# Block-sorted attention with a hypernetwork mixer: one batch turned by transposing transfers, and the order of all units laid out anew

## The chip, the cores and the metric

The kernel runs on one core of a Trainium2 chip. A core has a matrix engine (TensorE, PE in the profile; its weight loads are PEld), a vector engine (DVE), an activation engine (ACT), a general engine (GpSimd, POOL), a synchronisation engine (SyncE, SP) that here only issues transfers, and 16 DMA engines that all queues share. Each engine works through its own instructions in order and waits on semaphores for the others. The metric is device time in microseconds (us), the median of several executions; the profile is of one execution.

## What is computed

Inputs are q, k, v (4 batches, 8 heads, 768 positions, 64 wide), a sort_net of 8x8 for each batch and head, and three weight matrices. Cut to what matters:

```python
P = sort_net
for _ in range(5):                      # Sinkhorn
    P = exp(P - max(P, -1)); P /= sum(P, -1) + 1e-9; P /= sum(P, -2) + 1e-9
k_sorted = einsum('bhij,bhjcd->bhicd', P, k_blocks)     # 8 blocks of 96 rows
v_sorted = einsum('bhij,bhjcd->bhicd', P, v_blocks)
attn = softmax(q_b @ k_sorted_b.T / 8)                  # within each block
x = (attn @ v_sorted_b)                                 # 768 x 512 for each batch
wq, wk = x @ w_q, x @ w_k
mixed = (wq @ wk.T / 8) @ x
out = relu(mixed) @ w_out
```

## The kernel before

The program is a list of units, written out by hand in the string ORDER (L18 to L46). A loop at the end (L597 to L607) walks through the list and issues each unit's instructions, so the list fixes the order on every engine: an engine gets its units in the order in which they stand there. An item such as `K12:6` is read as follows: K is the kind of unit, 1 the batch, 2 the part (here a pair of heads), and 6 the first of the PSUM banks it uses (eight banks in all). Capital letters are matrix products on PE. Small letters that follow are the work of another engine on their result, with the engine named: `k12:D:6` is the copy of that result by DVE (D), A is ACT, G GpSimd, S SyncE. The kinds:

- `l`: loads, all issued by GpSimd with conversion to bf16 (L215): `lq0` is q of batch 0, `lp` the two small weights w_q and w_k (tile wqk, L208), `lo` the matrix w_out (tile wo, L210). There are three buffers each for q, k and v.
- `a`, `c`, `p`, `B`, `u`, `i`: the Sinkhorn iterations (a: exponential on ACT; c: sums and divisions on DVE), constants, and the spread of the result over partitions (tile PTR).
- `n`: M, the sorting matrices of a batch (L239). For batch 0 they are made on DVE from PSUM, two heads at a time; for the others on GpSimd from PTR, four heads at a time (`n10`, `n11`). There are two buffers of M, so batch 2 writes where batch 0 was, and batch 3 where batch 1 was.
- `Q`/`q`: q turned; `K`/`k`: k sorted and turned at once by products with M. Twelve small products in each.
- `V`/`v` and `R`: v sorted into tile Vs, then moved into place by six transfers from SBUF to SBUF on SyncE's queue (tile VT). For batch 0 another way is taken: `Y`/`y` sorts and turns, `F`/`f` turns back, with no transfer.
- `S`/`e`: scores and their exponential (seven units for each batch); `P`, then `r` and `x`: weights by values with the row sums, reciprocal, and division into tile X (five units).
- `T`/`t`: X turned on PE into PSUM and copied to tile XT, four units of eight products; each of the four parts is 96x1024 turned to 128x768. The function `u_D` (L356) does the same by one transposing transfer; no unit of the order before calls it.
- `J`/`j`, `d`: x by w_q and w_k in two halves, each taking all four parts of XT; `W`/`w` turns wk, `G`/`g` is wk by x, `H`/`h` the mixing with relu (tile mixT), `O`/`o` the product with w_out, `s` the store. The o units write four output buffers in turn, so an o waits until the store from that buffer has landed.
- `Z`: products on zeros that fill time on PE; `Z09:2` is nine of them.

Of the kernel before, what the change touches and what calls it, by code (L numbers as in the profile page):

```python
# [16 lines left out]
ORDER = """
i02:D Z03:0 lq0 c00:D lk0 a01:A c01:D i00:G i03:G B01:0 p01:A a02:A p00:A:0 c02:D lq1 lv0 a03:A c03:D lv1  # L18
Z010:0 lk1 a04:A c04:D lp a05:A c05:D lk2 Q03:0 lq2 Q02:1 q03:A:0 Q01:2 B00:3 lo q01:D:2 q02:A:1 Q00:0 n03:D:3
lv2 n01:D:3 K03:1 n02:D:3 K01:4 q00:D:0 k03:A:1 lq3 K02:6 n00:D:3 k01:A:4 k02:D:6 S05:0 u00:A:3 S02:4 e05:A:0  # L20
S03:6 n10:G S04:2 e02:A:4 Q13:0 Q11:1 n11:G q13:D:0 e03:A:6 K00:4 q11:D:1 Q10:0 k00:A:4 S06:6 lk3 Q12:1
e06:A:6 S00:4 q12:D:1 q10:A:0 S01:6 e01:A:6 Y03:0 y03:A:0 e04:A:2 Y01:6 Y00:0 y01:D:6 y00:A:0 n20:G F03:3
Z09:2 f03:A:3 e00:A:4 F01:0 F00:1 f01:D:0 V12:2 f00:D:1 Y02:4 v12:A:2 P04:6 n21:G P01:0 r04:D:6 y02:A:4
x04:D:6 P00:2 R15:S r01:D:0 R14:S lv3 K13:4 r00:D:2 x01:D:0 K11:6 k13:A:4 k11:D:6 K10:0 S16:4 x00:D:2 e16:A:4
V11:6 V10:4 v11:A:6 k10:D:0 T00:3 n30:G F02:2 v10:A:4 t00:D:3 R13:S S11:0 f02:D:2 K12:6 R12:S e11:A:0 S10:4
n31:G k12:D:6 R10:S P02:2 e10:A:4 P03:0 R11:S r02:D:2 x02:D:2 S13:6 K20:4 e13:A:6 r03:D:0 T01:2 x03:D:0
k20:A:4 S14:6 t01:D:2 e14:A:6 T03:0 K22:3 t03:A:0 K23:1 k22:D:3 S15:6 T02:5 e15:A:6 k23:D:1 Q23:4 Q20:3
q23:A:4 Q22:6 t02:D:5 q20:D:3 q22:A:6 S12:0 P13:6 e12:A:0 J00:5 r13:D:6 x13:D:6 P10:3 j00:A:5 S24:0 d00:G
W00:5 r10:D:3 e24:A:0 P14:6 x10:D:3 J01:2 S20:0 j01:D:2 S25:3 e20:A:0 r14:D:6 w00:D:5 d01:G W01:2 x14:D:6
Q21:5 e25:A:3 P11:0 q21:D:5 S26:6 w01:D:2 T13:5 r11:D:0 e26:A:6 x11:D:0 V22:2 t13:A:5 V21:6 v22:A:2 P12:4  # L30
v21:D:6 V20:0 T10:2 R24:S r12:D:4 G00:3 v20:D:0 t10:A:2 R23:S K21:6 R22:S G01:3 k21:A:6 x12:D:4 R21:S Q31:0
g00:A:3 Q33:1 R20:S q31:D:0 H00:2 S21:4 R25:S q33:D:1 H02:6 h00:A:2 T11:0 h02:D:6 e21:A:4 T12:1 S22:2 t12:D:1
H01:6 t11:A:0 S23:4 h01:D:6 O00:1 e22:A:2 J11:0 o00:A:1 e23:A:4 K32:6 j11:D:0 K31:1 k32:D:6 d11:G J10:3
k31:D:1 K33:4 j10:A:3 K30:6 W10:3 d10:D k30:A:6 O02:0 k33:D:4 w10:A:3 W11:7 o02:A:0 S36:5 S35:3 w11:D:7 S32:1
e36:A:5 G10:7 e35:A:3 P22:5 e32:A:1 G11:7 r22:D:5 x22:D:5 V32:3 P23:0 v32:A:3 O05:2 g10:D:7 r23:D:0 x23:D:0
R35:S H11:6 o05:A:2 H10:4 R34:S Q30:3 h11:A:6 h10:D:4 T22:0 V30:1 q30:A:3 P24:6 t22:D:0 O11:5 v30:A:1 r24:D:6
x24:D:6 S30:3 o11:D:5 Q32:0 R31:S e30:A:3 P21:6 R30:S P20:1 q32:A:0 r21:D:6 V31:3 x21:D:6 T23:5 v31:A:3 O03:0
r20:D:1 t23:D:5 x20:D:1 S34:6 R32:S o03:A:0 S33:4 T21:3 R33:S e33:A:4 O04:0 t21:D:3 s01:S e34:A:6 S31:1
o04:D:0 H12:3 T20:5 e31:A:1 h12:D:3 O10:6 s02:S P32:0 o10:D:6 P33:2 r32:D:0 O01:4 s10:S r33:D:2 x32:D:0 O15:6
x33:D:2 P34:0 o15:A:6 O14:7 t20:D:5 P31:2 o01:D:4 o14:A:7 J20:5 r31:D:2 s00:S r34:D:0 x34:D:0 J21:4 s12:S  # L40
j20:A:5 x31:D:2 T32:7 d20:G j21:A:4 W20:0 T33:1 d21:G W21:6 w20:D:0 T31:2 t33:D:1 w21:A:6 G20:0 t31:D:2 P30:5
t32:D:7 G21:0 r30:D:5 x30:D:5 O12:7 g20:A:0 H21:0 o12:A:7 H20:2 H22:4 h21:D:0 h20:A:2 T30:6 O13:7 t30:D:6
O22:3 h22:D:4 o13:A:7 J30:2 s11:S o22:A:3 J31:7 j30:D:2 O21:6 d30:D j31:A:7 d31:D W30:7 W31:5 o21:A:6 O23:4
w31:D:5 w30:A:7 G30:7 o23:A:4 O24:6 s21:S G31:7 o24:A:6 O20:4 g30:A:7 H32:6 o20:D:4 H31:1 h32:A:6 O25:5
h31:D:1 s20:S H30:3 o25:A:5 O35:7 h30:D:3 s22:S O34:6 o35:D:7 O31:5 o34:A:6 s35:S O32:7 s34:S o31:A:5 O30:6
s31:S o32:A:7 O33:5 s32:S o30:A:6 s30:S o33:A:5 s33:S  # L46
"""


# [595 lines left out]
```

## Time and profile before

| | |
|---|---|
| runs | 109.33, 109.36 and 109.76 us, median 109.36 |
| profiled execution | 109.27 us |
| its span from the first to the last instruction seen | 107.4 us |
| input read and output written | 20.19 MB and 6.29 MB |
| dummy products Z | 22 of 1475 matrix products |

The rows in the prediction come from several views: the head of the page; busy time by stretches; the order of time, where a row has start, duration, engine, line, operation, output and input tiles, count, and in brackets how long the engine stood idle ahead of it and what ended that; groups by line and shape, with busy us in all, then ns of one; and the transfers with KB of each and median us from issue to landing. A matmul's duration includes the time that it takes to run through the array, so what one costs in a dense stretch is read from the starts of successive rows, not from their durations.

### The profile page before, as it was taken

The page shows a single profiled execution, that of the slowest core. Times are in us where ns is not written, and L with a number is a line of the kernel's source. Part 1 is how long each engine was busy: PE and PEld are TensorE (multiplying, and loading weights), DVE is VectorE, ACT ScalarE, POOL GpSimd, SP SyncE. Part 2 cuts the span into 40 slices and gives each one's busy share as a digit, 9 for nine tenths or more (in the row PEclk, how much of TensorE's full clock was granted, in tenths as well). Part 3 has the DMA queues.
Part 4 walks back from the last instruction along what each step waited for, and adds up shares of the span by engine and source line. Part 5 has one row for each costly group of instructions (what it writes and reads, how often), then busy time and mean ns, then how long its engine had stood idle before and what let it go on. Part 6 is the DMA issues. An engine that isn't in the chain of part 4 may idle for free.

```text
span 107.4 us, 3466 instructions
## 1 busy us (share of the span) xinstructions
PE 91.2 (85%) x1475; PEld 61.4 (57%) x1486; DVE 72.3 (67%) x143; ACT 68.8 (64%) x99; POOL 28.4 (26%) x47
## 2 busy tenths in 40 slices
...
DMA  0999999999999999999999400323974503145982
GB/s 3 100 198 205 203 205 205 203 204 205 186 204 215 228 233 243 205 205 203 207 209 263 85 6 0 101 55 96 359 279 166 240 0 148 50 198 206 362 310 98
DMA packets 18879, 19.04 MB, mean 177 GB/s; under 512 B 1840, under 2 KB 16944, under 8 KB 18864
## 3 DMA queue, kind: packets, MB, share of 16 engines
...
q14 instruction: 4, 0.03, 0.1%
HBM read 20.19 MB, written 6.29 MB: 247 GB/s over the span
## 4 chain that ended last, share of the span: by engine, by line
PE 43%; DMA 24%; DVE 15%; POOL 8%; issue 4%; ACT 3%; DVEq 0%; SPq 0%; POOLq 0%; ACTq 0%
PE ps L143 43%; DMA Vn<-in_v_dram 17%; DMA VT<-Vs 7%; DVE X L344 6%; POOL M L239 2%; DVE mixT L410 2%; POOL Qn L215 2%; DVE Rall L339 1%; DVE Vs L149 1%; ACT Vs L147 1%; ACT E L315 1%; DVE ot L149 1%; POOL Kn L215 1%; DVE KT L149 1%; POOL Vn L215 1%
## 5 line engine op out<-in xcount | busy, mean ns | idle before, releaser
L315 ACT ACTIVATE E<-ps 96x960 bf16<-96x960 f32 (+1 forms) x28 | 24.4, 902 | 2.3 <-PE ps L143 2.1
L143 PE MATMUL ps<-wo,mixT 128*128 128x512 bf16 x86 | 22.4, 379 | 0.5
L344 DVE TENSOR_TENSOR X<-ps,Rall 96x896 bf16<-96x896 f32 (+1 forms) x20 | 19.8, 1000 | 0.4
L147 ACT COPY ot<-ps 128x512 f32<-128x512 f32 x18 | 10.6, 586 | 10.2 <-PE ps L143 10.1
L371 POOL COPY qD<-qkT 64x384 bf16<-64x384 bf16 x5 | 2.5, 503 | 43.9 <-ACT qkT L147 31.2
L143 PEld LDWEIGHTS <-mixT 128*128 128x128 bf16 x96 | 8.3, 98 | 8.6 <-issue 1.0
L143 PE MATMUL ps<-VT,E 96*128 96x65 bf16 x256 | 10.5, 193 | 1.3 <-DMA VT<-Vs 1.2
L149 DVE CAST KT<-ps 128x768 bf16<-128x768 f32 x10 | 9.4, 952 | 2.8 <-PE ps L143 2.8
L143 PEld LDWEIGHTS <-E 96*128 96x128 bf16 x256 | 9.3, 97 | 2.9 <-issue 1.7
L143 PE MATMUL ps<-fil 128*128 128x512 bf16 x21 | 9.1, 607 | 2.0 <-DVE fil L191 1.2
L143 PEld LDWEIGHTS <-KT 64*128 64x128 bf16 (+1 forms) x288 | 8.5, 98 | 4.1 <-issue 1.9
L147 ACT CAST KT<-ps 128x768 bf16<-128x768 f32 x10 | 7.9, 798 | 3.8 <-PE ps L143 3.7
L410 DVE TENSOR_SCALAR mixT<-ps 128x1024 bf16<-128x1024 f32 x8 | 9.8, 1222 | 0.5 <-PE ps L143 0.4
L147 ACT CAST Vs<-ps 128x1024 bf16<-128x1024 f32 x7 | 7.0, 1019 | 4.3 <-PE ps L143 3.8
L143 PE MATMUL ps<-QT,KT 64*128 64x96 bf16 x256 | 9.1, 204 | 0.5 <-ACT KT L147 0.5
L143 PE MATMUL ps<-idb,X 96*128 96x96 bf16 x128 | 8.0, 207 | 0.6 <-DVE X L344 0.6
L143 PE MATMUL ps<-idb,Qn 128*64 128x128 bf16 x192 | 7.5, 225 | 1.0 <-DMA Qn<-in_q_dram 0.9
L239 POOL TENSOR_TENSOR M<-PTR,m_p 128x512 bf16<-128x512 bf16 x6 | 7.8, 1310 | 1.3 <-PE ps L143 1.3
L143 PE MATMUL ps<-M,Kn 128*64 128x128 bf16 x192 | 7.2, 221 | 0.8 <-DVE X L344 0.4
L143 PEld LDWEIGHTS <-Qn 128*64 128x64 bf16 x192 | 6.2, 113 | 2.6 <-DMA Qn<-in_q_dram 1.9
L143 PEld LDWEIGHTS <-X 96*128 96x128 bf16 x128 | 6.2, 98 | 2.2 <-issue 0.6
L339 DVE RECIPROCAL Rall<-ps 96x14 f32<-96x14 f32 (+1 forms) x20 | 4.3, 223 | 4.7 <-PE ps L143 4.6
...
## 6 DMA issues: line engine op xcount, KB each, us to landing
out_dram<-ot SPq DMA_DIRECT2D x9, 512.0 KB, 2.8
Qn<-in_q_dram POOLq DMA_DIRECT2D x4, 768.0 KB, 18.5
Kn<-in_k_dram POOLq DMA_DIRECT2D x4, 768.0 KB, 22.2
Vn<-in_v_dram POOLq DMA_DIRECT2D x4, 768.0 KB, 21.8
VT<-Vs SPq DMA_DIRECT2D x18, 132.0 KB, 5.8
...
wo<-in_moe_w_out_dram POOLq DMA_DIRECT2D x1, 512.0 KB, 25.1
wqk<-in_moe_w_q_dram POOLq DMA_DIRECT2D x1, 64.0 KB, 20.6
```

The costliest lines, as they stand in the source:

```text
L143: nc.tensor.matmul(o, w, x, is_transpose=t, start=start, stop=stop, skip_group_check=True)
L147: nc.scalar.copy(o, i)
L149: nc.vector.tensor_copy(o, i)
L215: nc.gpsimd.dma_start(out=t[b % NIN][:, h0:h1].rearrange("p h r d -> p h (r d)"), in_=src[b, h0:h1].rearrange("h (p r) d -> p h (r d)", p=P))
L239: ENG[e].tensor_tensor(out=M[b % 2][:, h0:h0 + hn], in0=src.unsqueeze(2).to_broadcast([P, hn, SP, NB]), in1=m_p.unsqueeze(1).unsqueeze(3). ...
L315: nc.scalar.activation(E[b % 2][:, n, 0:2 * w * BLK].rearrange("p (t a c) -> p a t c", a=2, c=BLK), PS[0:BLK, bank:bank + 2, 0:w * BLK].re ...
L339: nc.vector.reciprocal(Rall[:, b, n, :, 0:w], avps(bank, w)[:, :, :, D])
L344: nc.vector.tensor_mul(xo.rearrange("p (a t d) -> p a t d", a=2, d=D), avps(bank, w)[:, :, :, 0:D], Rall[:, b, n, :, 0:w].unsqueeze(3).to_ ...
L371: nc.gpsimd.tensor_copy(o, i)
L410: nc.vector.tensor_relu(o, i)
```

## The change

Only ORDER changes. Three things differ in it. The units T30 to T33 and t30 to t33 are gone, and D30 to D33 on SyncE stand in their stead. The order of the units and loads, the engine of many copies, and the PSUM banks are all dealt out anew. There are 28 dummy products instead of 22. The lines that matter here:

```diff
-i02:D Z03:0 lq0 c00:D lk0 a01:A c01:D i00:G i03:G B01:0 p01:A a02:A p00:A:0 c02:D lq1 lv0 a03:A c03:D lv1
-Z010:0 lk1 a04:A c04:D lp a05:A c05:D lk2 Q03:0 lq2 Q02:1 q03:A:0 Q01:2 B00:3 lo q01:D:2 q02:A:1 Q00:0 n03:D:3
-lv2 n01:D:3 K03:1 n02:D:3 K01:4 q00:D:0 k03:A:1 lq3 K02:6 n00:D:3 k01:A:4 k02:D:6 S05:0 u00:A:3 S02:4 e05:A:0
-S03:6 n10:G S04:2 e02:A:4 Q13:0 Q11:1 n11:G q13:D:0 e03:A:6 K00:4 q11:D:1 Q10:0 k00:A:4 S06:6 lk3 Q12:1
...
-k20:A:4 S14:6 t01:D:2 e14:A:6 T03:0 K22:3 t03:A:0 K23:1 k22:D:3 S15:6 T02:5 e15:A:6 k23:D:1 Q23:4 Q20:3
-q23:A:4 Q22:6 t02:D:5 q20:D:3 q22:A:6 S12:0 P13:6 e12:A:0 J00:5 r13:D:6 x13:D:6 P10:3 j00:A:5 S24:0 d00:G
...
-j20:A:5 x31:D:2 T32:7 d20:G j21:A:4 W20:0 T33:1 d21:G W21:6 w20:D:0 T31:2 t33:D:1 w21:A:6 G20:0 t31:D:2 P30:5
-t32:D:7 G21:0 r30:D:5 x30:D:5 O12:7 g20:A:0 H21:0 o12:A:7 H20:2 H22:4 h21:D:0 h20:A:2 T30:6 O13:7 t30:D:6
-O22:3 h22:D:4 o13:A:7 J30:2 s11:S o22:A:3 J31:7 j30:D:2 O21:6 d30:D j31:A:7 d31:D W30:7 W31:5 o21:A:6 O23:4
...
+i02:D lq0 lv0 c00:D a01:A c01:D i00:G i03:G B01:0 a02:A Z014:1 p00:A:0 c02:D lk0 lv1 a03:A p01:A c03:D lq1 lk1
+a04:A c04:D Q02:1 lq2 Z03:0 Q01:0 a05:A c05:D Q03:2 Z03:7 q03:A:2 Q00:7 q02:A:1 q01:D:0 B00:2 q00:A:7 n03:D:2
+n01:D:2 Y03:0 n02:D:2 Y01:6 n00:D:2 y03:A:0 Y02:3 u00:D:2 y01:A:6 Y00:0 n10:G y02:A:3 y00:D:0 F01:7 F03:6
+n11:G f01:D:7 K01:0 f03:A:6 K00:2 k01:D:0 K02:4 lp K03:6 k02:A:4 k00:D:2 S02:0 e02:A:0 F00:4 k03:D:6 n21:G
...
+x03:D:2 V10:6 q12:A:0 x02:D:4 v10:A:6 Q10:1 T00:0 P04:2 q10:D:1 t00:A:0 R11:S K12:6 r04:D:2 x04:D:2 R15:S
+K13:4 Q11:0 k12:D:6 n31:G k13:A:4 R13:S Q13:1 K11:2 R10:S q13:D:1 T02:4 R14:S T03:7 lv2 t02:A:4 T01:1 t03:D:7
+R12:S Z08:6 t01:A:1 lo q11:A:0 k11:A:2 Q22:7 S16:0 S15:5 q22:D:7 e16:A:0 K10:2 e15:A:5 S13:0 n30:G J01:7
+e13:A:0 J00:5 j01:D:7 lk2 k10:A:2 S14:0 j00:D:5 Q21:7 e14:A:0 lq3 W00:5 q21:D:7 Q20:2 w00:D:5 S12:3 lv3 d00:D
+q20:D:2 W01:0 e12:A:3 V21:6 lk3 P13:1 w01:A:0 G00:5 v21:A:6 r13:D:1 d01:G x13:D:1 S11:3 G01:5 e11:A:3 S10:6
...
+W20:4 P32:0 w20:D:4 O12:5 o13:A:3 r32:D:0 x32:D:0 P31:6 o12:A:5 G20:3 r31:D:6 s11:S x31:D:6 H12:4 D32:S S30:0
+G21:3 e30:A:0 h12:D:4 O11:2 D31:S P34:0 o11:A:2 P30:6 r34:D:0 O14:4 g20:A:3 x34:D:0 r30:D:6 D33:S O10:0
+x30:D:6 o14:A:4 H21:1 o10:D:0 H22:3 D30:S H20:6 h21:A:1 O15:5 h20:D:6 h22:A:3 s10:S O23:0 o15:A:5 O21:7 s12:S
+J31:1 o21:A:7 J30:5 j31:A:1 O20:7 d31:G j30:A:5 o23:A:0 d30:G W30:5 O24:1 o20:D:7 w30:D:5 s20:S W31:7 o24:D:1
...
```

What the transposing unit issues, unchanged in the code:

```python
nc.sync.dma_start_transpose(out=XT[b % 2][:, n, :].rearrange("p (i c) -> p i c", i=NB),
                            in_=X[b % 2][:, n].rearrange("p i m -> p (i m)"))
```

More of the change, by code (lines that the diff above doesn't have):

```diff
@@ L17 @@
 ORDER = """
-i02:D Z03:0 lq0 c00:D lk0 a01:A c01:D i00:G i03:G B01:0 p01:A a02:A p00:A:0 c02:D lq1 lv0 a03:A c03:D lv1
-Z010:0 lk1 a04:A c04:D lp a05:A c05:D lk2 Q03:0 lq2 Q02:1 q03:A:0 Q01:2 B00:3 lo q01:D:2 q02:A:1 Q00:0 n03:D:3
-lv2 n01:D:3 K03:1 n02:D:3 K01:4 q00:D:0 k03:A:1 lq3 K02:6 n00:D:3 k01:A:4 k02:D:6 S05:0 u00:A:3 S02:4 e05:A:0
-S03:6 n10:G S04:2 e02:A:4 Q13:0 Q11:1 n11:G q13:D:0 e03:A:6 K00:4 q11:D:1 Q10:0 k00:A:4 S06:6 lk3 Q12:1
-e06:A:6 S00:4 q12:D:1 q10:A:0 S01:6 e01:A:6 Y03:0 y03:A:0 e04:A:2 Y01:6 Y00:0 y01:D:6 y00:A:0 n20:G F03:3
@@ L23 @@
[L23 to L26, printed above, removed]
-k20:A:4 S14:6 t01:D:2 e14:A:6 T03:0 K22:3 t03:A:0 K23:1 k22:D:3 S15:6 T02:5 e15:A:6 k23:D:1 Q23:4 Q20:3
@@ L28 @@
-q23:A:4 Q22:6 t02:D:5 q20:D:3 q22:A:6 S12:0 P13:6 e12:A:0 J00:5 r13:D:6 x13:D:6 P10:3 j00:A:5 S24:0 d00:G
[L29 to L37, printed above, removed]
@@ L38 @@
-r20:D:1 t23:D:5 x20:D:1 S34:6 R32:S o03:A:0 S33:4 T21:3 R33:S e33:A:4 O04:0 t21:D:3 s01:S e34:A:6 S31:1
-o04:D:0 H12:3 T20:5 e31:A:1 h12:D:3 O10:6 s02:S P32:0 o10:D:6 P33:2 r32:D:0 O01:4 s10:S r33:D:2 x32:D:0 O15:6
-x33:D:2 P34:0 o15:A:6 O14:7 t20:D:5 P31:2 o01:D:4 o14:A:7 J20:5 r31:D:2 s00:S r34:D:0 x34:D:0 J21:4 s12:S
-j20:A:5 x31:D:2 T32:7 d20:G j21:A:4 W20:0 T33:1 d21:G W21:6 w20:D:0 T31:2 t33:D:1 w21:A:6 G20:0 t31:D:2 P30:5
-t32:D:7 G21:0 r30:D:5 x30:D:5 O12:7 g20:A:0 H21:0 o12:A:7 H20:2 H22:4 h21:D:0 h20:A:2 T30:6 O13:7 t30:D:6
@@ L43 @@
-O22:3 h22:D:4 o13:A:7 J30:2 s11:S o22:A:3 J31:7 j30:D:2 O21:6 d30:D j31:A:7 d31:D W30:7 W31:5 o21:A:6 O23:4
-w31:D:5 w30:A:7 G30:7 o23:A:4 O24:6 s21:S G31:7 o24:A:6 O20:4 g30:A:7 H32:6 o20:D:4 H31:1 h32:A:6 O25:5
-h31:D:1 s20:S H30:3 o25:A:5 O35:7 h30:D:3 s22:S O34:6 o35:D:7 O31:5 o34:A:6 s35:S O32:7 s34:S o31:A:5 O30:6
-s31:S o32:A:7 O33:5 s32:S o30:A:6 s30:S o33:A:5 s33:S
+i02:D lq0 lv0 c00:D a01:A c01:D i00:G i03:G B01:0 a02:A Z014:1 p00:A:0 c02:D lk0 lv1 a03:A p01:A c03:D lq1 lk1
+a04:A c04:D Q02:1 lq2 Z03:0 Q01:0 a05:A c05:D Q03:2 Z03:7 q03:A:2 Q00:7 q02:A:1 q01:D:0 B00:2 q00:A:7 n03:D:2
@@ new lines @@
+n01:D:2 Y03:0 n02:D:2 Y01:6 n00:D:2 y03:A:0 Y02:3 u00:D:2 y01:A:6 Y00:0 n10:G y02:A:3 y00:D:0 F01:7 F03:6
+n11:G f01:D:7 K01:0 f03:A:6 K00:2 k01:D:0 K02:4 lp K03:6 k02:A:4 k00:D:2 S02:0 e02:A:0 F00:4 k03:D:6 n21:G
+S01:2 F02:5 e01:A:2 f00:D:4 S06:6 S04:0 n20:G f02:D:5 e04:A:0 S00:2 V12:4 e00:A:2 S05:0 v12:D:4 e06:A:6 P00:2
+e05:A:0 P01:6 r00:D:2 S03:4 x00:D:2 V11:0 e03:A:4 r01:D:6 P03:2 x01:D:6 v11:A:0 P02:4 r03:D:2 Q12:0 r02:D:4
+x03:D:2 V10:6 q12:A:0 x02:D:4 v10:A:6 Q10:1 T00:0 P04:2 q10:D:1 t00:A:0 R11:S K12:6 r04:D:2 x04:D:2 R15:S
@@ new lines @@
+K13:4 Q11:0 k12:D:6 n31:G k13:A:4 R13:S Q13:1 K11:2 R10:S q13:D:1 T02:4 R14:S T03:7 lv2 t02:A:4 T01:1 t03:D:7
+R12:S Z08:6 t01:A:1 lo q11:A:0 k11:A:2 Q22:7 S16:0 S15:5 q22:D:7 e16:A:0 K10:2 e15:A:5 S13:0 n30:G J01:7
+e13:A:0 J00:5 j01:D:7 lk2 k10:A:2 S14:0 j00:D:5 Q21:7 e14:A:0 lq3 W00:5 q21:D:7 Q20:2 w00:D:5 S12:3 lv3 d00:D
+q20:D:2 W01:0 e12:A:3 V21:6 lk3 P13:1 w01:A:0 G00:5 v21:A:6 r13:D:1 d01:G x13:D:1 S11:3 G01:5 e11:A:3 S10:6
+g00:D:5 P14:0 e10:A:6 H01:2 r14:D:0 V20:4 x14:D:0 h01:A:2 H00:6 P12:0 h00:A:6 O02:2 r12:D:0 x12:D:0 v20:A:4
```

13 lines of the change are left out of this document (added).

## The prediction

> **What bounds the kernel now.** I read the page's head first, then busy time by stretches of 5 us, then the order of time on TensorE and GpSimd, then what waited for whom.
>
> ```profile
> span 107.4 us, 3466 instructions
> PE 91.2 (85%) x1475; PEld 61.4 (57%) x1486; DVE 72.3 (67%) x143; ACT 68.8 (64%) x99; POOL 28.4 (26%) x47
> DMA  0999999999999999999999400323974503145982
> ```
>
> ```profile
> 15.00:20.00 5.00, 3.71 (x114) 3.04 (x114) 1.71 (x4) 4.84 (x8) 0.75 (x1) 1.00 1.32 204
> 20.00:25.00 5.00, 2.98 (x46) 2.28 (x48) 0.96 (x1) 4.16 (x6) 0.89 (x1) 0.85 1.32 205
> 25.00:30.00 5.00, 4.70 (x55) 2.96 (x54) 1.29 (x2) 1.64 (x3) 4.39 (x4) 0.81 1.50 195
> 40.00:45.00 5.00, 3.75 (x106) 3.24 (x104) 2.76 (x5) 4.29 (x6) 0.00 (x0) 1.00 1.24 227
> 50.00:55.00 5.00, 4.95 (x110) 4.56 (x111) 4.87 (x8) 4.04 (x6) 0.00 (x0) 1.00 1.32 205
> ```
>
> The columns after the stretch are busy us of PE, weight loads, DVE, ACT and POOL, then the granted clock. There are two regimes. From 45 us PE has hardly a gap (4.95 of 5). Before that it starves: DMA is full and loads arrive one at a time. So what counts is how much matmul work is done when the dense part begins, and how much is left. The boundary is the unit P13 (batch 1, weights by values):
>
> ```profile
> 40.84 0.39 PE L143 MATMUL ps<-QT,KT 64*128 64x96 bf16 x10
> 44.44 0.59 PE L143 MATMUL ps<-VT,E 96*128 96x65 bf16 x14 [1.23 <-DMA VT<-Vs]
> 98.05 5.35 PE L143 MATMUL ps<-wo,mixT 128*128 128x512 bf16 x23
> ```
>
> P13 starts at 44.44, after 1.23 us of waiting for batch 1's sorted V. The reason lies on GpSimd's queue, which carries both the loads and the multiplications n (L239) that make the sorting matrix M:
>
> ```profile
> 1.27 1.13 POOL L215 DMA_DIRECT2D Qn<-in_q_dram  x1 [0.82 <-POOLq L629]
> 2.40 0.89 POOL L215 DMA_DIRECT2D Kn<-in_k_dram  x1
> 5.82 1.76 POOL L215 DMA_DIRECT2D Vn<-in_v_dram  x2
> 25.31 0.88 POOL L215 DMA_DIRECT2D Qn<-in_q_dram  x1 [3.28 <-DMA Vn<-in_v_dram]
> 26.20 2.57 POOL L239 TENSOR_TENSOR M<-PTR,m_p 128x512 bf16<-128x512 bf16 x2
> ```
>
> Batch 1's M is made only at 26.20, because the load of q3 ahead of it waited 3.28 us for v1 to land; V1 and its VT transfers follow from there.
>
> **When loads land.** The views of the three input tiles give issue to landing (minimum, median, maximum; first Qn, then Kn, then Vn):
>
> ```profile
> DMA to landing us min/median/max: 7.7/18.5/25.2
> DMA to landing us min/median/max: 10.5/22.2/25.2
> DMA to landing us min/median/max: 15.0/21.8/27.3
> ```
>
> The minimum of each is its batch 0: q0 at 1.27+7.7 = 9.0, k0 at 2.40+10.5 = 12.9 and v0, the fourth load, at 5.82+15.0 = 20.8. So a load takes 3.95 us. The new order of loads is q0, v0, k0, v1, q1, k1, q2, wqk, v2, wo, k2, q3, v3, k3: v0 12.9, k0 16.9, v1 20.8, q1 24.8, k1 28.7, q2 32.7.
>
> ```profile
> wqk<-in_moe_w_q_dram POOLq DMA_DIRECT2D x1, 64.0 KB, 20.6
> Qn<-in_q_dram POOLq DMA_DIRECT2D x4, 768.0 KB, 18.5
> VT<-Vs SPq DMA_DIRECT2D x18, 132.0 KB, 5.8
> out_dram<-ot SPq DMA_DIRECT2D x9, 512.0 KB, 2.8
> ```
>
> By bytes the two halves of wqk cost 0.66 us (33.4), v2 another 3.95 (37.4), and batch 1's six VT transfers up to 6·132/768 of a load, 4.1 us. That puts v2 between 37.4 and 41.5. I take 40.5, since these transfers leave when v10 is done, about 29, and mostly run ahead of v2.
>
> **The change part by part.** *Early order.* n10 and n11 now stand ahead of every load that can wait, so V1 follows v1 (20.8) instead of a waiting load. The new order then runs load by load to V21, first user of v2. Engines allow about the same time. Between K12 (28.7 plus some 0.8 for its bank) and V21, ACT has six evacuations of 0.8, four exponentials and a short one:
>
> ```profile
> L315 ACT ACTIVATE E<-ps 96x960 bf16<-96x960 f32 x24 | 22.5, 971 | 1.6 <-PE ps L143 1.5
> L147 ACT CAST KT<-ps 128x768 bf16<-128x768 f32 x10 | 7.9, 798 | 3.8 <-PE ps L143 3.7
> ```
>
> 4.8+3.9+0.5 = 9.2, to 38.7 without a gap. So V21 starts at 40.5, bounds 38.7 and 42.5 (loads at their latest, plus 1 us of waits).
>
> What is done by then, against before at 44.44? Batch 0's attention and its T0, and V1, Q1, K1 and three of Q2, in both. The new order has J00, J01, W00, W01 more, and S11, S10 and three K2 less. Starts of successive PE rows price these:
>
> ```profile
> 73.49 0.60 PE L143 MATMUL ps<-QT,KT 64*128 64x96 bf16 x20
> 74.02 0.52 PE L143 MATMUL ps<-idb,X 96*128 96x96 bf16 x8
> 40.05 0.86 PE L143 MATMUL ps<-M,Kn 128*64 128x128 bf16 x24
> 81.25 1.46 PE L143 MATMUL ps<-XT,wqk 128*128 128x384 bf16 x8
> 82.55 0.51 PE L143 MATMUL ps<-idb,X 96*128 96x96 bf16 x8
> 82.89 0.39 PE L143 MATMUL ps<-idb,qkT 128*96 128x128 bf16 x4
> 83.11 0.51 PE L143 MATMUL ps<-idb,X 96*128 96x96 bf16 x8
> ```
>
> S is (74.02−73.49)/2 = 0.27, K (40.84−40.05)/2 = 0.40, J (82.55−81.25)/2 = 0.65, T 0.34, W 0.22. So 1.74 more against 1.74 less: equal work, reached 44.44−40.5 = 3.9 us sooner (bounds 1.9 and 5.7). The price after that point is taken as unchanged: engine letters and banks are dealt out anew, but DVE loses evacuations and ACT gains some, with the sum of both smaller. I bound this re-dealing by ±1 us, about one exponential's length of extra or saved wait.
>
> *Turning X3.* T30 to T33 leave PE: 4·0.34 = 1.4 us in the dense part, so on the path. Their four DVE copies leave too, 0.54 each, beside PE work:
>
> ```profile
> L149 DVE COPY XT<-ps 128x768 bf16<-128x768 bf16 x12 | 6.5, 544 | 0.2 <-PE ps L143 0.2
> L344 DVE TENSOR_TENSOR X<-ps,Rall 96x896 bf16<-96x896 f32 x16 | 17.2, 1079 | 0.3
> L344 DVE TENSOR_TENSOR X<-ps,Rall 96x512 bf16<-96x512 f32 x4 | 2.7, 684 | 0.1
> 77.96 1.89 PE L143 MATMUL ps<-wo,mixT 128*128 128x512 bf16 x8
> 79.69 0.41 PE L143 MATMUL ps<-VT,E 96*128 96x65 bf16 x8
> L301 SPq DMA_DIRECT2D VT<-Vs x18: 546/598/1452, 30.4 to 74.0; - x18
> DMA to landing us min/median/max: 2.3/5.8/7.6
> ```
>
> In their place SyncE issues D32, D31, D33, D30, each 96x1024 bf16, 196 KB. J31's first product reads the part that D30 writes. D30 waits for x30. From P30's start, DVE still has x34 (0.68) and x30 (1.08) with two short reciprocals, about 2.9 us after P30's start with its matmuls. PE meanwhile has P30, O14, O10, H21, H22, H20, O15, O23 and O21: five O at (79.69−77.96)/2 = 0.87, P30 and three H about 1.3, together 5.7. So D30 has 2.8 us of cover. No row here shows a transposing transfer. The nearest one from SBUF to SBUF on this queue is VT<-Vs, 2.3 us at its fastest for 132 KB, which by bytes makes 3.4; 2.3 would be hidden, 7.6 (its slowest, under full load) would stall 4.8. I take 3.4: 0.6 us of stall. It can't gain, for PE has other work. Behind J31 all of PE waits; behind D30 on SyncE stands s10, which frees the slot that o23 on ACT writes, with w31 and g30 behind that.
>
> [...]
>
> *Fillers.* The dummy products Z go from 22 to 28, all before 35 us where PE starves. They cost nothing while loads set the pace; without that cover, 0.2 to 0.4 us each.
>
> *Loads late in the order.* lv2 now stands behind n31 on GpSimd, which needs K12 and K13 (about 30.3) and takes 1.3: issue at 31.6, while q2 and wqk fill the queue to 33.4. No gap, margin 1.8 us. lk2 stands behind n30 (K10, about 36): 37.6, with v2 and wo still moving.
>
> **Sum.** Against the profiled execution, 109.27 us (its span 107.4, 1.87 around it): −3.9 −1.4 +0.6 = 104.6. It lies 0.09 under the median of the runs, 109.36, so 104.7. The tail behind PE (last copy, last store) stays as it is. Terms at their ends: −5.7−1.4−1.0 gives 101.3; −1.9−1.4+1.0 with no stall 107.1.
>
> **Rivals.** *The transfers queue up (slower).* If a transposing transfer holds the queue c us and the four run one after another, D30 ends 4c after D32's start, which stands six O (5.2) and about 2.3 us of S30, G21, P34, P30 and three H ahead of J31; the stall is 4c−7.5. With the gain of 5.3 this turns slower from c = 3.2. At the VT median, c = 5.8, the stall is 15.7 and the time 104.1+15.7 = 119.8. For it: nothing is measured for such a transfer, and 5.8 is what an SBUF to SBUF transfer took here. Against: those ran against full loads, several at once, and from 60 us on the DMA row shows mostly under half. [...] Chance 0.22.
> *Only D30 is late.* Latency up to 7.6 with overlap among the four: 104.1+4.8 = 108.9, middle 107. Chance 0.12.
> *The load-paced stretch slips.* PE in the gaps drops to the clock of the rows at 20 to 30 us (0.85, 0.81), where eight fillers took 3.21 us, 0.4 each, against 0.87/4 = 0.22 for the same shape later:
>
> ```profile
> 24.21 3.21 PE L143 MATMUL ps<-fil 128*128 128x512 bf16 x8 [0.22 <-issue]
> ```
>
> From K12 to V21 stand some 7 us of PE work; at 1.8 times that, V21 comes 5.6 us later, past its load, and lv2 misses its margin: 104.7+5.6 = 110.3, and half as much, 107.5, if the clock recovers midway. Against: 15 to 20 us kept 1.00 with 3.71 us busy, and the new order is denser there. Chance 0.11.
>
> **How the numbers follow.** Forecast 104.7, chance 0.55; its own range 101.3 to 107.1. All of it is faster by over 0.5% (0.55 us, about what a measurement of this kernel can tell from no change). The late D30 adds 0.11 faster and 0.01 same, the slipping stretch 0.03, 0.04 and 0.04, the queue 0.01 same and 0.21 slower: faster 0.69, same 0.06, slower 0.25. The range runs from 102.0 to 111.0 and leaves out most of the queueing case and a sliver below.
>
> **What would show it.** M of batch 1 made by 19 us; V21 near 40.5 and P13 without a VT wait; PE dense from there, last matmul near 98.5; D30 landing under 4 us after issue and J31 waiting less than 1 us. The early step is wrong if V21 starts after 43, or the clock is under 0.9 in 28 to 40 us. The forecast falls if SyncE issues the D's more than 3 us apart with x ready, or if J31 waits over 4 us.

## The result, and the profile after

| kernel | runs | median | ratio to before, 95% interval |
|---|---|---|---|
| before | 109.24 to 109.76 us | 109.34 us | |
| changed | 104.92, 105.29, 105.76, 107.26 us | 105.53 us | 0.962 [0.958, 0.966] |

The change makes the kernel 3.8 us faster by the medians; 104.7 had been forecast. The execution profiled with the result is the one of 107.26 us, in which the granted clock fell behind a wait of PE (first fence); ratios and times below leave such executions out (which leaves one of six for a1_T and c4_k0 and two of six for c3_s12 and d1_noZ8, and the traces of a1_T, c2_Dlast, c4_k0 and d1_noZ8 are of executions left out), and the same kernel, run once more as a0_same, is read from an undisturbed execution of 105.50 us.

The profiled execution of the changed kernel: one row of the order of time on PE, and two stretches (columns as before; the granted clock is the third number from the end).

```profile
40.72 0.61 PE L143 MATMUL ps<-Vn,M 128*128 128x128 bf16 x8 [1.91 <-DMA Vn<-in_v_dram]
```

```profile
40.00:45.00 5.00, 4.28 (x68) 3.17 (x69) 1.75 (x3) 2.59 (x3) 0.29 (x1) 0.73 1.29 207
45.00:50.00 5.00, 4.78 (x46) 2.76 (x44) 2.39 (x5) 3.31 (x4) 0.00 (x0) 0.59 1.31 202
```

In a0_same (line numbers of the kernels run as experiments are one or two lower, so L141 here is L143 in the rows of before) the same stretches and the ones shown of before read:

```profile
15.00:20.00 5.00, 4.49 (x102) 3.92 (x104) 4.55 (x6) 4.05 (x6) 4.99 (x6) 1.00 1.32 204
20.00:25.00 5.00, 4.18 (x106) 3.44 (x106) 3.98 (x7) 4.77 (x7) 1.15 (x1) 1.00 1.32 204
25.00:30.00 5.00, 4.08 (x113) 3.65 (x111) 4.94 (x9) 3.43 (x5) 0.33 (x1) 1.00 1.32 205
...
40.00:45.00 5.00, 4.35 (x84) 3.17 (x84) 2.65 (x5) 3.46 (x5) 0.17 (x1) 1.00 1.29 206
...
50.00:55.00 5.00, 4.82 (x115) 3.60 (x115) 3.89 (x7) 4.57 (x7) 0.00 (x0) 1.00 1.25 235
```

PE is busy 4.18 of 5 us between 20 and 25 us, where it was 2.98, and at the full clock, where it was 0.85. DMA is as full as before (1.32): the loads did not get faster, the work stands in a better order behind them. GpSimd's order of time in a0_same shows how:

```profile
14.46 2.58 POOL L237 TENSOR_TENSOR M<-PTR,m_p 128x512 bf16<-128x512 bf16 x2 [5.14 <-ACT KT L145]
...
30.93 0.95 POOL L213 DMA_DIRECT2D Vn<-in_v_dram  x1
```

M of batch 1 is made at 14.46, not 26.20, and lv2 is issued at 30.93. PE's order of time in a0_same, at the four places that matter:

```profile
40.65 0.61 PE L141 MATMUL ps<-Vn,M 128*128 128x128 bf16 x8 [1.50 <-DMA Vn<-in_v_dram]
41.09 0.60 PE L141 MATMUL ps<-VT,E 96*128 96x65 bf16 x14
...
59.70 0.60 PE L141 MATMUL ps<-VT,E 96*128 96x65 bf16 x14 [1.23 <-DMA VT<-Vs]
...
87.22 1.46 PE L141 MATMUL ps<-XT,wqk 128*128 128x384 bf16 x8 [1.21 <-DMA XT<-X]
...
93.60 6.27 PE L141 MATMUL ps<-wo,mixT 128*128 128x512 bf16 x28
```

V21 starts at 40.65 behind v2, P13 follows without a wait, the first P of batch 2 waits 1.23 us for its VT transfers, and J31 waits 1.21 us for D30. From the boundary to PE's end, one stretch of each kernel, first before, then a0_same:

```profile
44.44:103.44 59.00, 57.98 (x846) 37.93 (x856) 45.18 (x73) 38.99 (x58) 5.75 (x12) 1.00 0.63 168
```

```profile
40.65:99.87 59.22, 56.05 (x856) 36.91 (x863) 40.89 (x66) 42.24 (x60) 5.20 (x11) 1.00 0.81 193
```

So the dense part is as long as it was (59.22 against 59.00): PE has 1.93 us less to do in it, and stands idle 3.17 us instead of 1.02. In lengths, the gain of 3.7 us in span (103.7 against 107.4) is the 3.8 us by which the dense part begins sooner. That does not make the transfers worth nothing: c1_T2 below begins its dense part as early and turns X3 on PE, and its dense part is longer.

### The profile page after: what moved, and what is told of

Same layout as the page of the kernel before. It is cut to its first block, busy times and chain, and to the rows that moved or that the text cites. A ratio compares the mean times of both kernels' runs of the same rounds, so it can differ in the third digit from the quotient of the medians.

```text
span 105.5 us, 3413 instructions
## 1 busy us (share of the span) xinstructions
PE 90.5 (86%) x1450; PEld 61.0 (58%) x1460; DVE 68.6 (65%) x138; ACT 70.4 (67%) x100; POOL 28.4 (27%) x47
## 4 chain that ended last, share of the span: by engine, by line
PE 49%; DMA 33%; POOL 6%; ACT 3%; issue 3%; DVE 2%; POOLq 0%; DVEq 0%
PE ps L143 49%; DMA Kn<-in_k_dram 20%; DMA Vn<-in_v_dram 9%; DMA XT<-X 4%; ACT E L315 2%; DVE X L344 2%; POOL Vn L215 2%; POOL Qn L215 1%; POOL M L239 1%; POOL Kn L215 1%; ACT ot L147 1%; POOL E L196 0%; DVE Rall L339 0%; POOL idb L187 0%; POOL VT L202 0%
## 5 line engine op out<-in xcount | busy, mean ns | idle before, releaser
L315 ACT ACTIVATE E<-ps 96x960 bf16<-96x960 f32 (+1 forms) x28 | 23.8, 899 | 3.7 <-PE ps L143 3.6
L143 PE MATMUL ps<-wo,mixT 128*128 128x512 bf16 x88 | 22.9, 386 | 0.7 <-issue 0.5
L143 PEld LDWEIGHTS <-mixT 128*128 128x128 bf16 x96 | 8.5, 99 | 9.4 <-issue 1.4
L147 ACT COPY ot<-ps 128x512 f32<-128x512 f32 x15 | 8.8, 587 | 6.3 <-PE ps L143 4.1
L143 PE MATMUL ps<-VT,E 96*128 96x65 bf16 x256 | 11.1, 197 | 0.9 <-ACT E L315 0.7
L149 DVE COPY ot<-ps 128x512 f32<-128x512 f32 x9 | 6.1, 683 | 8.6 <-PE ps L143 8.5
L143 PEld LDWEIGHTS <-E 96*128 96x128 bf16 x256 | 9.8, 100 | 2.9 <-issue 1.4
L143 PEld LDWEIGHTS <-KT 64*128 64x128 bf16 (+1 forms) x288 | 8.6, 99 | 3.9 <-issue 2.2
L147 ACT CAST KT<-ps 128x768 bf16<-128x768 f32 x12 | 9.4, 807 | 1.7 <-PE ps L143 1.7
L408 ACT ACTIVATE mixT<-ps 128x1024 bf16<-128x1024 f32 x8 | 8.1, 1024 | 3.3 <-PE ps L143 3.2
L143 PE MATMUL ps<-QT,KT 64*128 64x96 bf16 x256 | 9.5, 209 | 0.1
L149 DVE CAST KT<-ps 128x768 bf16<-128x768 f32 x8 | 7.5, 955 | 2.2 <-PE ps L143 2.2
L143 PE MATMUL ps<-fil 128*128 128x512 bf16 x26 | 8.2, 468 | 0.2 <-issue 0.2
L143 PE MATMUL ps<-idb,Qn 128*64 128x128 bf16 x192 | 7.9, 221 | 0.2 <-ACT Vs L147 0.2
L143 PE MATMUL ps<-M,Kn 128*64 128x128 bf16 x192 | 7.2, 221 | 0.7 <-DMA Kn<-in_k_dram 0.7
L149 DVE COPY QT<-ps 128x768 bf16<-128x768 bf16 x11 | 6.0, 549 | 2.7 <-PE ps L143 2.6
L143 PE MATMUL ps<-Vn,M 128*128 128x128 bf16 x72 | 5.9, 229 | 1.9 <-DMA Vn<-in_v_dram 1.9
```

Source lines behind the costliest of these rows:

```text
L143: nc.tensor.matmul(o, w, x, is_transpose=t, start=start, stop=stop, skip_group_check=True)
L147: nc.scalar.copy(o, i)
L149: nc.vector.tensor_copy(o, i)
L315: nc.scalar.activation(E[b % 2][:, n, 0:2 * w * BLK].rearrange("p (t a c) -> p a t c", a=2, c=BLK), PS[0:BLK, bank:bank + 2, 0:w * BLK].re ...
L408: nc.scalar.activation(o, i, ACT.Relu)
```

## Experiments

The kernel before was run beside them each time, with medians of 109.36 to 109.61 us.

**a0_same**, the changed kernel again.

> The changed kernel once more, so that the others have it beside them. Mean of its undisturbed runs near 105.3 us. If its profile has the clock at 1.00 from 40 to 50 us, the idle time of PE ahead of V21 (1.9 us in the first profile) and the wait for D30 (about 1.3 us) should be there all the same, for they come from transfers and not from the clock.

Measured: 105.11 to 106.16 us, median 105.66, ratio 0.964 [0.960, 0.968]. The waits for v2 (1.50 us) and for D30 (1.21 us) are there at the full clock, as expected. The result stands, and this is the measure for the variants below.

**a1_T**, the transposes of the last batch put back on PE, with one bank:

```diff
-H12:4 D32:S S30:0
+H12:4 T32:2 t32:D:2 S30:0
...
-H22:3 D30:S H20:6 h21:A:1 O15:5
+H22:3 H20:6 h21:A:1 T30:2 t30:D:2 O15:5
```

> The changed kernel with X of the last batch turned on PE again (T30 to T33 and their four copies on DVE), everything else as it is. My theory: PE gets 1.4 us of work back and loses the wait of 1.2 to 1.4 us for D30, so the time is within 0.7 us of the changed kernel (104.6 to 106.0), and J31 no longer waits for a transfer. The rival, that the transposing transfers carry a good part of the gain: 1.4 us slower or more. The rival, that they cost: over 0.7 us faster.

Measured: 108.24 us, one execution. It does not tell the theories apart, for my choice of bank 2 made a wait of its own:

```profile
85.45 0.28 PE L141 MATMUL ps<-qD,Ab 64*128 64x256 bf16 x1 [1.02 <-DVE XT L147]
```

H21 writes banks 1 and 2 and had to wait until the copy t33 had emptied bank 2. c1_T2 below does it with other banks.

**b1_D**, the order of before with T3 and t3 alone replaced by the four transfers:

```diff
-T32:7 d20:G j21:A:4 W20:0 T33:1 d21:G W21:6 w20:D:0 T31:2 t33:D:1
+D32:S d20:G j21:A:4 W20:0 D33:S d21:G W21:6 w20:D:0 D31:S
...
-h20:A:2 T30:6 O13:7 t30:D:6 O22:3
+h20:A:2 D30:S O13:7 O22:3
```

> The kernel before with the four transposing transfers alone, its order otherwise kept. In its profile x30 ends at 86.76 and the first unit that needs D30 starts at 89.58, which leaves 2.8 us, and T30 leaves that stretch, so D30 at 3 to 4.3 us stalls PE by 0.5 to 1.9 us, against 1.4 us of PE work saved. My theory: within 0.8 us of 109.3. If the transfers carry the change: 107.9 or less. If they queue up one after another: over 110.

Measured: 111.19 us, ratio 1.014 [1.011, 1.016], 1.4% slower. The expectation of no change within 0.8 us missed. The first J of batch 3 in PE's order of time:

```profile
91.93 1.46 PE L141 MATMUL ps<-XT,wqk 128*128 128x384 bf16 x8 [2.45 <-DMA XT<-X]
```

D30 was issued at 87.6, 1.9 us ahead of the end of the products that cover it, and took 4.3 us. The time lies where the queueing theory had put it (over 110), but the transfers did not queue: the one issued just ahead of D30 landed in 2.7 us. So the transfers alone are a loss where their cover is short; what makes D30 take 4.3 us is taken up below.

**a2_V21**, V21 put behind P13, G00 and S11 so that PE has work while v2 is still on its way:

```diff
-V21:6 lk3 P13:1 w01:A:0 G00:5 v21:A:6 r13:D:1 d01:G x13:D:1 S11:3 G01:5 e11:A:3 S10:6
+lk3 P13:1 w01:A:0 G00:5 r13:D:1 d01:G x13:D:1 S11:3 V21:6 e11:A:3 G01:5 v21:A:6 S10:6
```

> The changed kernel with V21 moved behind P13, G00 and S11, which need no load. If PE's idle stretch ahead of V21 is lost time on the path, as I hold, these 1.3 us of work fill it and the time falls by 0.8 to 1.5 us; the clock should also drop less often. If the stretch behind V21 is paced by ACT or by later loads, nothing changes (within 0.4 us).

Measured: 105.20 us, ratio 0.961 [0.958, 0.964]: 0.5 us below a0_same's 105.66, less than expected, and with intervals that overlap. The wait for v2 is gone, but half of it comes back one bank later:

```profile
42.91 0.39 PE L141 MATMUL ps<-QT,KT 64*128 64x96 bf16 x10 [0.85 <-ACT Vs L145]
```

S10 uses the bank that V21 has just filled and waits for ACT to empty it.

**c1_T2**, T30 to T33 on PE in other banks, two of the copies on ACT, and O15 ahead of J31:

```diff
-H12:4 D32:S S30:0
+H12:4 T32:2 t32:D:2 S30:0
...
-r30:D:6 D33:S O10:0 x30:D:6 o14:A:4
+r30:D:6 O10:0 T33:5 x30:D:6 t33:A:5 o14:A:4
...
-H22:3 D30:S H20:6 h21:A:1 O15:5
+H22:3 H20:6 T30:5 t30:D:5 h21:A:1
```

> The changed kernel with X of the last batch turned on PE, a second time: the first such kernel put three of the turns into banks that H21 and the relu copies wanted, and PE waited 1 us on a copy there, which says nothing of the transfers. Here the turns go to banks 2 and 5, two copies go to ACT, and O15 moves behind O21. My theory: 1.4 us more PE work against 1.2 to 1.4 us less waiting for D30, so within 0.8 us of the changed kernel's undisturbed runs (105.6), and no wait of J31 for a transfer. If the transfers carry part of the gain: 107 or more with PE free of waits there.

Measured: 107.96 us, ratio 0.986 [0.979, 0.992]. My theory, within 0.8 us of the changed kernel, missed. With the new order kept, the transfers are worth 2.3 us by the medians (107.96 to 105.66), not the forecast's 0.8, though the width of the interval leaves some 0.7 us either way. In the trace the last block of O starts at 95.50, against 93.60. Both traces stand at the same unit at 77.45; from there to that block PE is busy 16.81 us here and 14.58 in a0_same, and idle 1.24 and 1.57. Of the 2.23 us of busy time 1.4 are what the forecast gave the T's. Part of the idle time is that the last mixing comes late behind the copies on DVE and ACT:

```profile
85.78 1.04 PE L142 MATMUL ps<-wo,mixT 128*128 128x512 bf16 x3 [0.43 <-ACT mixT L407]
87.20 1.90 PE L142 MATMUL ps<-wo,mixT 128*128 128x512 bf16 x8 [0.38 <-DVE mixT L409]
88.94 1.65 PE L142 MATMUL ps<-XT,wqk 128*128 128x384 bf16 x8
```

These two waits, 0.8 us together, stand in place of the 1.21 us for D30. Where the T's were put back is my choice, so part of the 2.3 may belong to it.

**c2_Dlast**, all four transfers issued one behind the other after x30:

```diff
-r30:D:6 D33:S O10:0 x30:D:6 o14:A:4 H21:1 o10:D:0 H22:3 D30:S H20:6
+r30:D:6 O10:0 x30:D:6 D30:S D32:S D31:S D33:S o14:A:4 H21:1 o10:D:0 H22:3 H20:6
```

> The changed kernel with all four transposing transfers issued back to back once x30 is done (D30, D32, D31, D33). It measures the cost of one behind another. If only the issue on SyncE is serial (1.23 us each in the profiles so far), the fourth lands 3 to 4 times 1.23 later than D30 alone, some 90.5 to 91.5 on the clock of the undisturbed profile, J31 and J30 wait 2.5 to 4 us longer, and the time is 108 to 109.5. If each holds the path until it has landed (2.7 to 3 us, the rival of my prediction), the fourth lands at 94 or later and the time is 112 or more.

Measured: 109.58 us, ratio 1.000 [0.995, 1.004]. XT's transfers (durations of the issue on SyncE in ns, first and last issue), and the first J products on PE:

```profile
L355 SPq DMA_TRANSPOSE XT<-X x4: 1241/1310/1749, 84.5 to 89.1; - x4
...
DMA to landing us min/median/max: 2.6/3.0/3.9
```

```profile
88.46 0.32 PE L141 MATMUL ps<-XT,wqk 128*128 128x384 bf16 x1 [0.68 <-DMA XT<-X]
90.57 0.48 PE L141 MATMUL ps<-XT,wqk 128*128 128x384 bf16 x2 [1.79 <-DMA XT<-X]
91.83 1.52 PE L141 MATMUL ps<-XT,wqk 128*128 128x384 bf16 x5 [0.77 <-DMA XT<-X]
```

The four are issued 1.5 us apart ((89.1−84.5)/3), and land at 88.4, 89.3, 90.6 and 91.7, 1.1 us apart on average (the first of them late by itself, 3.9 us after its issue). The price in a row is c = 1.1 to 1.5 us, as the theory of a serial issue has it and far from the 3.2 at which the queueing rival turns slower and the 5.8 at which it was priced. Even so the row costs the whole gain of 3.9 us. In this trace, of an execution of 111.35 us, 2.0 of that are waits (3.24 us instead of 1.21), and behind them the clock falls (next fence); what makes up the rest is not shown. So it is not the transfers' speed but their place, each as soon as its x is there, that makes them cheap.

```profile
92.00:92.50 0.50, 0.50 (x4) 0.24 (x3) 0.00 (x0) 0.26 (x1) 0.00 (x0) 0.61 0.96 393
92.50:93.00 0.50, 0.50 (x3) 0.30 (x2) 0.00 (x0) 0.22 (x1) 0.22 (x1) 0.50 0.97 393
```

**c3_s12**, the store s10 taken from behind D30 and put behind s12, to see whether the 512 KB store slows D30:

```diff
-s10:S O23:0 o15:A:5 O21:7 s12:S J31:1
+O23:0 o15:A:5 O21:7 s12:S s10:S J31:1
```

> The changed kernel with the store s10 behind s12. In the profiles, D31 and D33 land 2.7 us after issue with nothing beside them, and D30 takes 4.3 with the 512 KB store s10 issued 1.3 us behind it. s12 needs o15, about 2 us later, so now no store runs beside D30. Theory A (the store slows it): D30 lands in 3.0 or less, J31's wait falls from 1.2 to under 0.3 us, and the time falls by up to 1 us unless o23, which needs s10, is late. Theory B (the transfers slow one another, D33 being 1.3 us ahead): D30 stays at 4.2 or more and J31's wait stays.

Measured: 104.94 and 105.38 us. The next store now leaves at 85.36 instead of 84.14, and nothing changes: D30 takes 4.3 us as before, and

```profile
87.15 1.46 PE L141 MATMUL ps<-XT,wqk 128*128 128x384 bf16 x8 [1.14 <-DMA XT<-X]
```

The store is not the cause; theory B's reason, D33 ahead of it, is put to the test further down.

**c4_k0**, k0 loaded ahead of v0, as in the old order:

```diff
-lq0 lv0 c00:D
+lq0 lk0 c00:D
...
-c02:D lk0 lv1
+c02:D lv0 lv1
```

> The changed kernel with k0 loaded ahead of v0 as in the order before, the units left as they are. Y03 then starts 3.5 us later (about 17 instead of 13.4). If the stretch to V21 is paced by k1, q2 and v2, as I hold, most of this is absorbed where PE waits for them (0.7 us ahead of K12, 1.5 to 1.9 ahead of V21) and the time grows by 0.5 to 2 us. If the early chain carries through: 3 us or more. If v0 early was worth nothing: within 0.4 us.

Measured: 107.29 us in one execution, 1.6 above a0_same and inside the expected 0.5 to 2; the trace is of another, of 111.71 us, so its lengths show the mechanism and not what the swap costs in time. GpSimd's rows, a stretch, and V21 in its profile:

```profile
33.01 1.31 POOL L237 TENSOR_TENSOR M<-PTR,m_p 128x512 bf16<-128x512 bf16 x1 [8.23 <-PE ps L141]
34.27 0.95 POOL L213 DMA_DIRECT2D Vn<-in_v_dram  x1
```

```profile
30.00:35.00 5.00, 4.90 (x128) 4.43 (x124) 4.84 (x8) 3.83 (x5) 1.99 (x2) 1.00 1.02 145
```

```profile
44.44 1.01 PE L141 MATMUL ps<-Vn,M 128*128 128x128 bf16 x8 [2.24 <-DMA Vn<-in_v_dram]
```

PE starts on the sort of v0 at 16.37 after 2.70 us of waiting, and all that follows slides: n31 and with it lv2 come 3.3 us later (34.27 against 30.93). Of this some 0.8 us is the clock, 0.67 between 15 and 20 us in this execution: the 48 products of the sort took 2.53 us, against 1.73 in a2_V21. That is more than the margin of 1.8 us that the forecast gave lv2, and the queue does run dry: 145 GB/s between 30 and 35 us, where a0_same moved 230, and from 33.5 to 36.0 the loads' queue moves nothing at all, while in a0_same v2's packets begin at 34.0, within half a microsecond of wqk's last. V21 starts 3.8 us later. The margin is also smaller than it was put: here v2's first packets move 1.7 us after its issue begins (36.0 and 34.27), so of a0_same's, issued at 30.93 with the queue at work until about 33.5, some 0.8 us is left.

**What makes D30 slow.** In each trace so far one of the four transposing transfers took 3.9 to 4.4 us, D30 each time, first or last of the four, and the others 2.6 to 3.3 (the first of b1_D, beside a store, 4.1; of d3_bDnoZ9 below, with the same order there, 4.2). The view of the DMA queues, a0_same from 83 to 84 us, names a second queue (packets, MB, share of 16 engines):

```profile
q1 hardware_dynamic: 494, 0.12, 53.2%
q8 instruction: 1, 0.02, 10.5%
```

The packet of the instruction queue moves 0.02 MB and lasts 0.105·16 = 1.7 us on one DMA engine. Narrowed to a tenth of a microsecond, it starts at 83.7 in a0_same and c3_s12 (D30 issued 82.8, 4.4 and 4.3 us), at 84.2 in a2_V21 (D30 issued 82.6, 4.3), at 88.4 in b1_D (D30 issued 87.6, 4.3), and at 85.4 in c2_Dlast (D30 issued first, 84.5, 3.9).

In steps of 0.2 us the same view shows what the delay is made of. In d2_V21noZ8 below, with no instruction packet near, the 800 packets of D30 move in one go, from 84.0 to 85.2. In a0_same 501 of them have moved by 84.8. Then nothing moves until 85.4, when the instruction packet ends (83.7 + 1.7). From there to 86.2 only 28 follow, with little more than one of the 16 engines busy (7.7 to 9.1%), and the rest come behind them. The other four traces show the same trickle, and in each it begins as the packet ends. So it looks as if the transfer waited for one engine that the packet held; the view does not name the engine, and the times alone are measured.

A run has eleven such packets for 2910 products and weight loads of PE, one for some 265 of them in the mean (2910/11); from the first packet to the last of the execution profiled first, 17.2 to 85.8 us, it is one for some 240 (2403/10). The view gives the queue's name and not what its packets bring. That they bring PE its instructions, so that with fewer of these ahead a packet comes later, was the author's estimate from this count. The next runs test it, by taking instructions away ahead of the packet.

**d1_noZ8**, the changed kernel without eight dummy products, and **d2_V21noZ8**, a2_V21 without them:

```diff
-R12:S Z08:6 t01:A:1
+R12:S t01:A:1
```

> The changed kernel without the eight dummy products Z08 that stand ahead of Q11's copy, near 32 us; nothing else. Why: in four traces the transposing transfer that lands 3.9 to 4.4 us after its issue, and not 2.7, is the one beside which a packet of the instruction queue (0.02 MB, 0.9 to 1.7 us on one DMA engine) moves: at 83.7 us in the changed kernel, in D30's transfer. Eleven such packets for some 2900 instructions of PE and its weight loads look like one packet per 256 of them. Sixteen instructions fewer put the packet sixteen of them later, two output products or 1.7 us, near 85.5, behind D30. Theory F (instruction fetch): D30 lands 2.7 to 3.0 us after its issue, J31 waits under 0.3 us instead of 1.2, and the time is 104.4 to 104.8 in undisturbed runs against 105.65. Theory R (D30 is slow because it is issued 1.3 us behind D33, or last): D30 4.3, J31's wait 1.2, time 105.3 to 106. Fillers: the forecast has them at nothing under the loads' cover, and 0.2 us each where that cover is gone, so 0 to 1.7 us gained ahead of V21; if they hold the clock up instead, PE's clock between 33 and 50 us drops below 0.8 and the time is over 107.

> a2_V21 (V21 behind P13, G00 and S11) without the same eight dummy products. There the instruction packet lay at 84.2 us and D30 took 4.3 us, J31 waited 1.1. Theory F: packet near 86, D30 2.7 to 3.0 us, J31's wait under 0.3, time 103.9 to 104.3 against a2_V21's 105.2. Theory R: D30 4.3, wait 1.1, time 105.0 to 105.5. If the fillers hold the clock up, over 106.5.

Measured: d1_noZ8 104.37 and 105.56 us, ratio 0.960 [0.955, 0.964]; d2_V21noZ8 103.53 us, ratio 0.946 [0.944, 0.947]. In d2_V21noZ8 the packet starts at 86.1, D30 issued at 82.9 lands 2.7 us later, and J31 follows without a wait; J31's row and XT's transfers:

```profile
85.92 1.46 PE L141 MATMUL ps<-XT,wqk 128*128 128x384 bf16 x8
```

```profile
L355 SPq DMA_TRANSPOSE XT<-X x4: 1212/1234/1380, 78.3 to 82.9; - x4
...
DMA to landing us min/median/max: 2.7/2.7/3.3
```

d1_noZ8 shows the same (packet 88.1, D30 2.7 us, J31 without a wait). The time of d1_noZ8 does not decide, for one execution lies in each theory's range; the landings and the wait do, and d2_V21noZ8's time is 1.7 us below a2_V21's, more than forecast. The theory of the instruction packet holds; that D30 is slow because it comes last or close behind D33 falls, for both are as they were. The fillers themselves are no cost under the loads: without Z08, 1.67 us of dummy products, PE waits 1.06 us for q2 in their place, and the first J starts at 35.23, where it started at 35.29 in a2_V21. But they do something else. Behind that wait and one of 0.39 us for wqk d2_V21noZ8 runs at a lower clock:

```profile
35.00:40.00 5.00, 4.77 (x56) 2.73 (x56) 2.01 (x5) 2.69 (x4) 4.93 (x6) 0.66 1.27 221
```

**d3_bDnoZ9**, b1_D without its dummy products Z09:

```diff
-F03:3 Z09:2 f03:A:3
+F03:3 f03:A:3
```

> b1_D (the order of before with T3 and t3 replaced by the four transposing transfers, 111.24) without the dummy products Z09 near 25 us. In b1_D the instruction packet lay at 88.4 us, in D30's transfer (issue 87.6, 4.3 us), and J30 waited 2.45 us. Eighteen instructions fewer put it past the wait. Theory F: D30 2.7 to 3.0 us, J30's wait 0.7 to 1.2, time 109.6 to 110.1. Theory R: D30 4.3, wait 2.4, time 111 to 111.5. Taking the fillers away may move the early part by up to 1 us either way, so the wait and the landing decide, and the time only behind them.

Measured: 111.09 us, ratio 1.015 [1.011, 1.018]. The wait came as the packet theory has it, 0.77 us:

```profile
91.57 1.46 PE L141 MATMUL ps<-XT,wqk 128*128 128x384 bf16 x8 [0.77 <-DMA XT<-X]
```

The time missed: Z09 was worth its place. PE's first P of batch 0, 36 products at 30 us, took 2.16 us without it, and 1.31 in b1_D; the clock was 0.50 from 25 to 30 us and 0.64 from 30 to 35, against 0.93 and 1.00. What was won at J30 was lost there.

**e1_Z8kept**, a2_V21 with Z08 kept and eight earlier dummy products taken out:

```diff
-a02:A Z014:1 p00:A:0
+a02:A Z012:1 p00:A:0
...
-lq2 Z03:0 Q01:0 a05:A c05:D Q03:2 Z03:7 q03:A:2
+lq2 Q01:0 a05:A c05:D Q03:2 q03:A:2
```

> a2_V21 with Z08 kept, and eight other dummy products taken out instead: both Z03 (10 to 12 us) and two of the fourteen of Z014 ahead of q0's landing. Again sixteen PE instructions fewer ahead of D30, so by theory F the instruction packet lies near 86 us as in d2_V21noZ8, D30 lands in 2.7 to 3.0 us, J31 waits under 0.3. What differs is where PE idles: with Z08 kept it has no gap near 33 us, after which d2_V21noZ8 ran its first J product at half the clock (8 products in 2.74 us instead of 1.46). If Z08 is worth its place, the clock stays over 0.99 in most runs and the median is 103.3 to 104.0, against 104.48; if the small gaps at 10 to 12 us cost the clock instead, the stretch 10 to 20 us shows under 0.9 and the median is over 104.5.

Measured: 103.97 us, ratio 0.952 [0.948, 0.956], with J31 at 85.06 without a wait (packet at 85.2, D30 issued at 82.0 and landed 2.7 us later). The clock is now 1.00 from 20 us on and 0.78 between 15 and 20. So moving the packet pays again, and the gap with its lower clock only changes its place: the time is in the range expected if Z08 is worth its place, the clock from 15 to 20 us is what was expected if the early gaps cost it, and without Z08 the kernel is 0.4 us faster still. Both versions beat the changed kernel, d2_V21noZ8, the fastest of the study, by 2.1 us and this one by 1.7.

## Why the prediction was right

The terms of the sum, in spans of the profiled executions (107.4 and 103.7):

| term | forecast | measured in a0_same |
|---|---|---|
| dense part begins sooner (V21 against P13) | −3.9 | −3.8 (44.44 to 40.65) |
| T3 leaves PE, re-dealing | −1.4, ±1 | −1.9 of PE work |
| J31 waits for D30 | +0.6 (0 to 4.8) | +1.2 |
| other idle time of PE in the dense part | 0 | +0.9 |
| tail behind PE | 0 | −0.1 |
| sum | −4.7 | −3.7 |

- *Order of loads.* Right, and the trace shows the steps: M of batch 1 by 17 us, wqk's packets through at about 33.5 (33.4 forecast), the VT transfers mostly ahead of v2, V21 at 40.65 where 40.5 was forecast, waiting for v2 and not for an engine. That it came so near is in part luck, for the 40.5 was chosen by judgement between 37.4 and 41.5. c4_k0 undoes one swap: V21 slides by 3.8 us in its trace, and the one time there is for it is 1.6 us longer. It also shows that lv2 has a margin that can be used up. Moving n10 and n11 ahead of the waiting loads was not tested alone.
- *Equal work at the boundary, and a dense part of the same price.* This missed by 1.0 us, the whole error of the sum. By the forecast the dense part would have been 58.2 us (59.0 − 1.4 + 0.6); it is 59.2, for what the T's left free was spent on waits. The step that failed is "the price after that point is taken as unchanged": P of batch 2 waits 1.23 us at 59.70 for its VT transfers, which the forecast did not look for: it asked what V21 waits for, not what follows V21. Why they are late is open. They hang on v2 through V20 to V22. But they also run beside the last loads: issued from 47.2 to 52.1, they land 5.9 to 7.3 us later, where the first three of batch 3, issued behind the loads at 61.9 to 63.6, take 2.6 to 3.4. In d2_V21noZ8 V22 runs 0.9 us later than here (49.61 against 48.70) and this P starts at the same time, 59.77. That speaks for the loads; no run separates the two.
- *D30.* The mechanism was right and its size too small, 1.2 us against 0.6: 4.4 us to land with 3.2 of cover, against 3.4 with 2.8. Both signs set for it (landing under 4 us, a wait under 1 us) were missed. The estimate by bytes, 3.4 us, lies above what such a transfer takes alone (2.7) and below what D30 took (4.4), for a reason that was not in the profile's rows that I read: the instruction packet. With the packet moved, the wait is zero.
- *T against D.* The forecast's net of 0.8 was too small in the new order (2.3 by c1_T2, some of it perhaps my placing) and of the wrong sign in the old one (b1_D, 1.6 us slower). So the split of the gain was off, too: the order alone, c1_T2 against before, is worth 1.4 us, not 3.9. Cover is part of the difference: in the new order 3.2 us of products stand between D30's issue (82.8) and J31 (86.0 without a wait), in the old one 1.9, and the waits are 1.21 and 2.45. These 1.2 us are a third of the way from 2.3 won to 1.6 lost; the rest is not traced.
- *Transfers that queue up.* Fell by c2_Dlast: c = 1.1 to 1.5 us. A transposing transfer of 196 KB landed 2.7 us after its issue (D30 in d2_V21noZ8), beside 2.6 at best for 132 KB of VT in a0_same.
- *The slipping stretch.* Its place was wrong for the changed kernel: between 28 and 40 us the clock stayed at 1.00. The clock fell behind V21's wait, from 40 to 50 us, in the execution profiled first. Without Z08 it does fall in that stretch (0.66 from 35 to 40 us in d2_V21noZ8).
- *Fillers at nothing.* Right for PE's time under the loads, wrong as a rule: d3_bDnoZ9 loses by the lower clock what it wins at J30.
